# Attention and two feed-forward layers on one core: earlier splits at a pair's end, and a new division of work in the first attention batch

## The chip, the cores and the metric

The kernel runs on one core of one Trainium2 chip. The metric is device time in microseconds (us) of one execution. Engines are named as in the profile: PE is TensorE (PEld its weight loads), DVE is VectorE, ACT is ScalarE, POOL is GpSimd, SP issues the plain DMAs.

## The reference

```python
def phi(x):                                   # random features, both for q and for k
    proj = einsum('bhsd,md->bhsm', x, omega)
    h = proj - sum(x * x) / 2
    return exp(h - max(h)) / sqrt(m)
q_p, k_p = phi(q * scale), phi(k * scale)     # 4 batches, 8 heads, 576 tokens, 64 -> 128 features
kv, z = einsum('bhsm,bhsd->bhmd', k_p, v), sum(k_p, axis=2)
x = einsum('bhsm,bhmd->bhsd', q_p, kv) / (einsum('bhsm,bhm->bhs', q_p, z) + 1e-06)
x = softplus(x @ w_in) @ w_out                # 2304 tokens, 512 -> 2048 -> 512
for e in range(8):                            # each token goes to its best expert, 512 -> 1024 -> 512
    out[mask] = gate * (relu(x[mask] @ w1[e]) @ w2[e])
```

## The kernel before

**Three stages.** Attention feeds the first feed-forward layer, which takes the tokens in six groups of 384; the attention of later batches is woven between the matmuls of the first groups. The expert layer follows, from about 620 us on.

**Splitting.** Most matmuls work on two parts of a number: a rounded high part and the rest. A split is two instructions: ACT writes the high part (a cast), then DVE subtracts it from the source and writes the low part. A product is then three matmuls: high by high, high by low, low by high.

**Attention.** Work comes in items of two 128-token pieces of two heads. `u` is the half of the heads (0 or 1), `b` the batch. Stage T transposes the input and splits it (`xThi`, `xTlo`), stage P multiplies by the features (`pp`) and takes the negated row maxima (`nm`), then makes the exponentials. `TUNE['exp_k']`, one letter for each `2*b + u`, says how for the keys: with 'a', ACT makes one exponential for each 128 columns with the maximum as its bias; with 'v', DVE adds the maxima to all columns, and ACT makes one exponential over them:

```python
if TUNE["exp_" + kind][2 * b + u] == "v":
    nc.vector.tensor_tensor(out=pe[:, :2 * n], in0=ph, in1=bc(nm[:, :2 * n].unsqueeze(2), [P, 2 * n, M]),
                            op=ALU.add)
    nc.scalar.activation(out=pe[:, :2 * n], in_=pe[:, :2 * n], func=AF.Exp)
else:
    for i in range(2 * n):
        nc.scalar.activation(out=pe[:, i, :], in_=pp[:, i * M:i * M + M], func=AF.Exp, bias=nm[:, i:i + 1])
```

Stage K sums the keys by values in `kv`, and stage N multiplies the queries' features by that into `nd`: 64 rows of `nd` are numerators and 64 denominators. ACT copies the denominators to `den` (L401), and `move("nx", ...)` copies the numerators to `xf` (L252 on ACT, L254 on DVE, by `TUNE['nx']`). Stage M divides: ACT makes the reciprocal `rc`, POOL multiplies, DVE corrects (L433). The first feed-forward group (`h`, L638) waits for the `x` that this writes.

**What sets the order there.** The attention's and the feed-forward's instructions are placed by a scheduler that has its own idea of durations; each engine then runs its own list strictly in order. The order in which DVE and ACT come to their work is thus fixed when the kernel is built.

**The expert layer** is a sequence of units in an order written out by hand (all but the first). A pair unit treats two 128-token slots of one expert, a single unit one. Units 4, 6, 8, 10, 12 and 14 are pairs, and each is followed by a single. Within a unit, the code also splits the next unit's weights: `w1_(c)` splits chunk c of `w1` (128x1024, in four chunks) into the buffers that chunk c of the present unit held, `w2_(c)` one of eight of `w2`. `pair_m1(g, k)` makes a fourth of the hidden values (L1365), `split(*hidden(k), ...)` applies relu and splits them (L1241, L1242), `pair_m2(g, k)` multiplies them into the output `po` (L1376), `unit_x(g + 1)` transposes and splits the next unit's tokens (`pt_x`, `mx`), `unit_out` scales (`ot`) and writes out. A single unit begins with `slot_m1(g, 0)` (L1343): it takes the high parts of the four chunks first, each for the two parts of the tokens, then the low parts of the four chunks. L1246 is the cast of a split, L1250 its subtraction, for weights and tokens alike.

Of the kernel before, what the change touches and what calls it, by code (L numbers as in the profile page):

```python
# [24 lines left out]
    kvs='aaaaaaaa',  # L25
    zc='aaaaaaaa',
    nd='aaavvaaa',
    nx='aavaaaaa',
    xh='aapaaaaa',
    qt='vvaaaaaa',  # L30
    exp_k='vaaavaaa',
    exp_q='vavvaavv',
    xl='pppppppp',
    den='sssssvvv',
# [42 lines left out]
def tile_kernel(ctx, tc, q, k, v, omega, w_in, w_out, emb, tau, w1, w2, out):  # L77
# [1138 lines left out]
    def fetch_w(s, which="12", chain=0):  # L1216
        for nm, src in (("w1r", w1v), ("w2r", w2v)):
            if nm[1] not in which:
                continue
            if s < 2:  # L1220
                raw_w[nm, s] = mraw.tile([P, NC * F2], F32, name=f"{nm}{s}")
            with tc.issue_after(marks["x"]) if chain and "x" in marks and s < 4 else ExitStack():
                nc.gpsimd.indirect_dma_start(
                    out=raw_w[nm, s % 2], out_offset=None, in_=src,
                    in_offset=bass.IndirectOffsetOnAxis(ap=w_idx[:, s:s + 1].bitcast(U32), axis=0),
                    bounds_check=E * P - 1, oob_is_err=False)

    def fetch_x(g):
        t = xpool.tile([P, 2, YW], F32, tag="xhi", name="xg")
        for i, s in enumerate(groups[g]):  # L1230
            nc.gpsimd.indirect_dma_start(
                out=t[:, i, :], out_offset=None, in_=(ya if s < NS_A else yb)[:, :],
                in_offset=bass.IndirectOffsetOnAxis(ap=g_idx[:, s:s + 1].bitcast(U32), axis=0),
                bounds_check=NT - 1, oob_is_err=False)
            xgs[s] = t[:, i, :]
            if s >= NS_A:
                marks["x"] = traced()

    def split(hi, lo, lo_eng, src, relu=False, hi_eng="a"):
        if relu:  # L1240
            nc.scalar.activation(out=hi, in_=src, func=AF.Relu)  # L1241
            nc.vector.scalar_tensor_tensor(out=lo, in0=src, scalar=0.0, in1=hi.bitcast(F32),  # L1242
                                           op0=ALU.max, op1=ALU.subtract)
        else:
            if hi_eng == "a":
                nc.scalar.copy(out=hi, in_=src)  # L1246
            else:
                (nc.gpsimd if hi_eng == "p" else nc.vector).tensor_copy(hi, src)
            eng = nc.gpsimd if lo_eng == "p" else nc.vector
            eng.tensor_tensor(out=lo, in0=src, in1=hi.bitcast(F32), op=ALU.subtract)  # L1250
# [55 lines left out]
    def unit_w1(g, c):  # L1306
        if (g, c) in w1s:
            return
        r = raw_w["w1r", g % 2][:, c * F2:(c + 1) * F2]
        t = [wpool.tile([P, F2], F32R, tag=f"wi{2 * c + i}", name=f"w1_{c}_{i}") for i in range(2)]  # L1310
        if len(groups[g]) == 1:
            o, r = [x.rearrange("q (h p c) -> q h p c", h=2, c=4) for x in t], \
                r.rearrange("q (p h c) -> q h p c", h=2, c=4)
        else:

            o, r = [x.rearrange("q (k p j) -> q k p j", k=4, j=2) for x in t], \
                r.rearrange("q (p k j) -> q k p j", k=4, j=2)
        kind = 0 if g < 2 else len(groups[g])
        split(*o, TUNE["w1"][kind][c], r, hi_eng=TUNE["w1h"][kind][c])
        w1s[g, c] = t  # L1320

    def unit_w2(g, c):
        if (g, c) in w2s:
            return
        r = raw_w["w2r", g % 2][:, c * DM:(c + 1) * DM]
        w2s[g, c] = [wpool.tile([P, DM], F32R, tag=f"wo{2 * c + i}", name=f"w2_{c}_{i}") for i in range(2)]
        split(*w2s[g, c], TUNE["w2"][g >= 2][c], r, hi_eng=TUNE["w2h"][g >= 2][c])
# [3 lines left out]
    def hidden(key):  # L1331
        hs[key] = [ring.tile([P, 512], F32R, tag=f"wo{x}", name=f"mh_{x}") for x in "hl"]
        return hs[key]

    def slot_m1(g, half, part=slice(0, 12)):
        if part.start == 0:
            hs["ps", half] = mpsum("h", "ph")
        ph = hs["ps", half]
        w = slice(half * HF, half * HF + HF)
        mms = [(xs[g][a][c], w1s[g, c][b_][:, w]) for c, (a, b_) in first_order(half)]  # L1340
        for i in range(part.start, part.stop):
            x, r = mms[i]
            nc.tensor.matmul(ph, lhsT=x, rhs=r, start=(i == 0), stop=(i == 3 * NC - 1))  # L1343
# [14 lines left out]
    def pair_m1(g, k):  # L1358

        ph = hs["ps"] = mpsum("h", "ph")  # L1360
        order = first_order(k)
        for n, (c, (a, b_)) in enumerate(order):
            for j in range(2):
                f = slice(2 * k * P + j, 2 * (k + 1) * P, 2)
                nc.tensor.matmul(ph[:, j * 256:j * 256 + 256], lhsT=w1s[g, c][b_][:, f],  # L1365
                                 rhs=xs[g][a][c].rearrange("p i t -> p (i t)"),
                                 start=(n == 0 and j == 0), stop=(n == len(order) - 1), skip_group_check=True)

    def unit_m2(g, i, parts):

        s = groups[g][i]
        if parts[0][2] == 0:
            po[s] = mpsum("o", "po")
        for h, o, c in parts:
            for n, (a, b_) in enumerate(PASSES):
                nc.tensor.matmul(po[s], lhsT=h[a][:, o:o + P], rhs=w2s[g, c][b_], start=(c == 0 and n == 0),  # L1376
                                 stop=(c == 7 and n == 2))

    def slot_m2(g, half, cs):
        unit_m2(g, 0, [(hs[half], c * P, 4 * half + c) for c in cs])  # L1380

    def pair_m2(g, k):
        for i in range(2):
            unit_m2(g, i, [(hs[k], 256 * j + P * i, 2 * k + j) for j in range(2)])

    def unit_out(g):
        for s in groups[g]:
            xt = xgs.pop(s)
            ot = xpool.tile([P, DM], F32, tag="xlo", name="ot")
            nc.scalar.activation(out=ot, in_=po.pop(s), func=AF.Copy, scale=xt[:, DM:YW])  # L1390
            nc.gpsimd.indirect_dma_start(  # L1391
                out=out, out_offset=bass.IndirectOffsetOnAxis(ap=s_idx[:, s:s + 1].bitcast(U32), axis=0),
                in_=ot, in_offset=None, bounds_check=NT - 1, oob_is_err=False)

    def unit(g):
        nxt = g + 1 < NG_ALL
        ahead = g + 2 < NG_ALL

        def w1_(*cs):
            for c in cs:  # L1400
                if nxt:
                    unit_w1(g + 1, c)

        def w2_(*cs):
            for c in cs:
                if nxt:
                    unit_w2(g + 1, c)

        def fetch():
            if ahead:  # L1410
                fetch_x(g + 2)
                fetch_w(g + 2, "2", 1)

        def own(*cs):
            for c in cs:
                unit_w2(g, c)

        if ahead:
            fetch_w(g + 2, "1", 1)
        if len(groups[g]) == 2:  # L1420
            pair_m1(g, 0)
            own(2, 3, 4)
            split(*hidden(0), "v", hs["ps"], relu=True)
            pair_m1(g, 1)
            own(5)
            split(*hidden(1), "v", hs["ps"], relu=True)
            pair_m2(g, 0)
            pair_m1(g, 2)
            own(6, 7)
            fetch()  # L1430
            w2_(0)
            split(*hidden(2), "v", hs["ps"], relu=True)
            pair_m2(g, 1)
            pair_m1(g, 3)
            w2_(1, 2, 3)
            split(*hidden(3), "v", hs["ps"], relu=True)
            pair_m2(g, 2)
            if nxt:
                unit_x(g + 1)
            w1_(0, 1, 2, 3)  # L1440
            pair_m2(g, 3)
            unit_out(g)
            w2_(4, 5)
        else:
            if g > 0:
                slot_m1(g, 0)
            own(2, 3, 4)
            slot_relu(0)
            slot_m1(g, 1, slice(0, 5))
            own(5)  # L1450
            slot_t(0)
            slot_m1(g, 1, slice(5, 12))
            own(6, 7)
            slot_relu(1)
            slot_m2(g, 0, (0, 1))
            w1_(0)
            slot_t(1)
            slot_m2(g, 0, (2, 3))
            if nxt:
                unit_x(g + 1)  # L1460
            w1_(1, 2, 3)
            slot_m2(g, 1, (0, 1))
            if g == 2:
                tokens(bm_b, NT_T, NS_A, NS_B, mpsum("o", "Lb"))
            fetch()
            slot_m2(g, 1, (2, 3))
            unit_out(g)
            w2_(0, 1)
# [127 lines left out]
```

## Time and profile before

| | |
|---|---|
| runs, us | 946.91, 940.6, 940.16 (median 940.6) |
| profiled execution, us | 942.76 |
| its span from first to last instruction, us | 940.9 |
| PE busy | 891.9 us (95%) |
| DVE, ACT, POOL busy | 689.8, 652.8, 323.0 us |

The span is what the rows below divide up; the profiled execution's own time has 1.9 us more around it, and it lies 2.2 us above the median of the runs. Busy shares over the whole span hide the stages, so the rows below are taken by stretch.

### The profile page before, as it was taken

The page shows a single profiled execution, that of the slowest core. Times are in us where ns is not written, and L with a number is a line of the kernel's source. Part 1 is how long each engine was busy: PE and PEld are TensorE (multiplying, and loading weights), DVE is VectorE, ACT ScalarE, POOL GpSimd, SP SyncE. Part 2 cuts the span into 40 slices and gives each one's busy share as a digit, 9 for nine tenths or more (in the row PEclk, how much of TensorE's full clock was granted, in tenths as well). Part 3 has the DMA queues.
Part 4 walks back from the last instruction along what each step waited for, and adds up shares of the span by engine and source line. Part 5 has one row for each costly group of instructions (what it writes and reads, how often), then busy time and mean ns, then how long its engine had stood idle before and what let it go on. Part 6 is the DMA issues. An engine that isn't in the chain of part 4 may idle for free. (4 is left out here: it accounts for less than half of the span.)

```text
span 940.9 us, 14526 instructions
## 1 busy us (share of the span) xinstructions
PE 891.9 (95%) x4951; PEld 744.5 (79%) x4951; DVE 689.8 (73%) x1376; ACT 652.8 (69%) x1452; POOL 323.0 (34%) x341
## 2 busy tenths in 40 slices
PE   6898899999999999998999999999999999999993
PEld 6775555588898889987888889888797888988972
DVE  6769888477888887679886777767977676685772
ACT  4897344477878877775877687876867576585672
POOL 1224102155545754575653020012243242241310
PEclk9899999999999999999999999999999999999998
DMA  6625663011362231011301381102023660551910
GB/s 165 166 76 152 185 217 113 17 35 37 57 146 72 45 93 35 20 35 23 68 7 23 81 344 46 34 12 57 26 65 142 276 243 30 211 209 41 356 58 6
DMA packets 86540, 94.69 MB, mean 101 GB/s; under 512 B 50294, under 2 KB 74870, under 8 KB 84160
## 3 DMA queue, kind: packets, MB, share of 16 engines
q1 hardware_dynamic: 77888, 45.21, 18.5%
q0 software_dynamic: 8576, 48.52, 13.7%
q8 instruction: 41, 0.67, 0.3%
q14 instruction: 35, 0.29, 0.1%
HBM read 108.36 MB, written 15.48 MB: 132 GB/s over the span
## 5 line engine op out<-in xcount | busy, mean ns | idle before, releaser
L1376 PE MATMUL po<-w,mh_h 128*128 128x512 f32 x368 | 118.0, 402 | 0.5 <-ACT mh_h L1354 0.5
L1250 DVE TENSOR_TENSOR w<-w2r,w 128x512 fp32r<-128x512 f32 x136 | 88.4, 684 | 17.5 <-ACT w L1246 17.5
L703 PE MATMUL y<-woh,gh 128*128 128x512 f32 x240 | 96.2, 408 | 1.7 <-DVE gh L682 1.7
L1246 ACT CAST w<-w2r 128x512 fp32r<-128x512 f32 x136 | 78.7, 628 | 23.3 <-DMA w2r<-in_moe_w_dram,w_idx 12.8
L703 PE MATMUL y<-wol,gh 128*128 128x512 f32 x240 | 93.9, 395 | 0.0
L1391 POOL DMA_INDIRECT out_dram<-ot,s_idx x23 | 31.5, 1369 | 171.0 <-ACT ot L1390 126.5
L1250 DVE TENSOR_TENSOR w<-w1r,w 128x1024 fp32r<-128x1024 f32 x68 | 80.4, 1226 | 11.1 <-ACT w L1246 11.0
L703 PE MATMUL y<-woh,gl 128*128 128x512 f32 x240 | 81.7, 404 | 0.0
L598 DVE TENSOR_TENSOR wil<-win,wih 128x512 fp32r<-128x512 f32 x72 | 58.4, 811 | 29.1 <-ACT wih L597 28.9
L1376 PEld LDWEIGHTS po<-w,mh_h 128*128 128x128 f32 x368 | 66.9, 191 | 12.2 <-ACT mh_h L1354 0.7
L638 PE MATMUL h<-xhi,wih 128*128 128x384 f32 x320 | 73.0, 348 | 3.2 <-DVE t L657 2.9
L1246 ACT CAST w<-w1r 128x1024 fp32r<-128x1024 f32 x68 | 72.0, 1119 | 3.5 <-PE ph L1343 2.1
L1376 PE MATMUL po<-w,mh_l 128*128 128x512 f32 x184 | 73.4, 399 | 0.9 <-DVE mh_l L1356 0.9
L610 POOL TENSOR_TENSOR wol<-wout,woh 128x512 fp32r<-128x512 f32 x40 | 55.0, 1376 | 45.3 <-ACT woh L609 45.2
L638 PE MATMUL h<-xlo,wih 128*128 128x384 f32 x320 | 70.2, 337 | 0.0
L638 PE MATMUL h<-xhi,wil 128*128 128x384 f32 x320 | 69.9, 339 | 0.0
L1365 PE MATMUL ph<-mxh,w 128*128 128x256 f32 x384 | 62.6, 285 | 0.4
L638 PEld LDWEIGHTS h<-xhi,wih 128*128 128x128 f32 x320 | 55.4, 188 | 8.3 <-DVE t L657 3.7
L425 POOL TENSOR_TENSOR xf<-xf,rc 128x256 f32<-128x256 f32 (+1 forms) x20 | 17.3, 867 | 122.0 <-ACT rc L424 114.8
L638 PEld LDWEIGHTS h<-xhi,wil 128*128 128x128 f32 x320 | 57.7, 188 | 0.3
L1365 PEld LDWEIGHTS ph<-mxh,w 128*128 128x128 f32 x384 | 55.0, 195 | 2.9 <-ACT w L1246 1.6
L638 PEld LDWEIGHTS h<-xlo,wih 128*128 128x128 f32 x320 | 56.4, 188 | 0.0
(311 smaller groups left out, 2376.6 us busy)
## 6 DMA issues: line engine op xcount, KB each, us to landing
wst<-in_moe_w_in_dram SPq DMA_DIRECT2D x16, 512.0 KB, 4.5
wst<-in_moe_w_out_dram SPq DMA_DIRECT2D x16, 512.0 KB, 4.3
raw<-in_k_dram SPq DMA_DIRECT2D x32, 128.0 KB, 2.4
vf<-in_v_dram SPq DMA_DIRECT2D x64, 64.0 KB, 2.3
raw<-in_q_dram SPq DMA_DIRECT2D x32, 128.0 KB, 2.6
ya<-yt SPq DMA_DIRECT2D x20, 128.2 KB, 4.4
yb<-yt SPq DMA_DIRECT2D x20, 128.2 KB, 4.0
ya<-yt SPq DMA_DIRECT2D x8, 256.5 KB, 5.7
```

Of the source, the lines that this page charges most:

```text
L425: nc.gpsimd.tensor_tensor(out=xf, in0=xf, in1=rc, op=ALU.mult)
L598: feng("il", n).tensor_tensor(out=il, in0=wi, in1=ih.bitcast(F32), op=ALU.subtract)
L610: feng("ol", n).tensor_tensor(out=ol, in0=wo, in1=oh.bitcast(F32), op=ALU.subtract)
L638: nc.tensor.matmul(h[:, 0:G], lhsT=a[:, c, :], rhs=x[:, c, :], start=(i == 0), stop=(i == last))
L703: nc.tensor.matmul(y, lhsT=x[:, c], rhs=w, start=(f == 0 and i == 0), stop=(f == NF - 1 and i == len(passes) - 1))
L1246: nc.scalar.copy(out=hi, in_=src)
L1250: eng.tensor_tensor(out=lo, in0=src, in1=hi.bitcast(F32), op=ALU.subtract)
L1365: nc.tensor.matmul(ph[:, j * 256:j * 256 + 256], lhsT=w1s[g, c][b_][:, f], rhs=xs[g][a][c].rearrange("p i t -> p (i t)"), start=(n == 0 an ...
L1376: nc.tensor.matmul(po[s], lhsT=h[a][:, o:o + P], rhs=w2s[g, c][b_], start=(c == 0 and n == 0), stop=(c == 7 and n == 2))
L1391: nc.gpsimd.indirect_dma_start(out=out, out_offset=bass.IndirectOffsetOnAxis(ap=s_idx[:, s:s + 1].bitcast(U32), axis=0), in_=ot, in_offset ...
```

## The change

Two letters-in-a-table edits and one reordering. In batch 0, the numerators of both halves of the heads are copied by DVE instead of ACT (`nx`), and the maxima of the second half's keys are added by DVE (`exp_k`), so that ACT makes one exponential where it made four. At a pair's end, the next unit's first chunk of `w1` is split ahead of the last hidden split, the second ahead of the next unit's tokens, and the third and fourth where all four stood.

```diff
-    nx='aavaaaaa',
+    nx='vvvaaaaa',
...
-    exp_k='vaaavaaa',
+    exp_k='vvaavaaa',
...
             pair_m1(g, 3)
             w2_(1, 2, 3)
+            w1_(0)
             split(*hidden(3), "v", hs["ps"], relu=True)
             pair_m2(g, 2)
+            w1_(1)
             if nxt:
                 unit_x(g + 1)
-            w1_(0, 1, 2, 3)
+            w1_(2, 3)
             pair_m2(g, 3)
             unit_out(g)
             w2_(4, 5)
```

ACT's list at the end of a pair unit (the second one), before. `w2r` and `w1r` are the raw weights of the next unit, `mh_h` the high part of the hidden values, `mx` that of the next unit's tokens:

```order
L1246 CAST w_1_0_10240<-w2r_6603 128x512
L1246 CAST w_2_0_10244<-w2r_6603 128x512
L1246 CAST w_3_0_10248<-w2r_6603 128x512
L1241 ACTIVATE mh_h<-ph 128x512
L1246 CAST mx<-pt_x 128x512
L1246 CAST w_0_0_10276<-w1r_6599 128x1024
L1246 CAST w_1_0_10280<-w1r_6599 128x1024
L1246 CAST w_2_0_10284<-w1r_6599 128x1024
L1246 CAST w_3_0_10288<-w1r_6599 128x1024
```

The same place on ACT after the change:

```order
L1246 CAST w_1_0_10232<-w2r_6595 128x512
L1246 CAST w_2_0_10236<-w2r_6595 128x512
L1246 CAST w_3_0_10240<-w2r_6595 128x512
L1246 CAST w_0_0_10244<-w1r_6591 128x1024
L1241 ACTIVATE mh_h<-ph 128x512
L1246 CAST w_1_0_10264<-w1r_6591 128x1024
L1246 CAST mx<-pt_x 128x512
L1246 CAST w_2_0_10276<-w1r_6591 128x1024
L1246 CAST w_3_0_10280<-w1r_6591 128x1024
```

One cast of `w1r` now stands ahead of the last relu, and one between it and the tokens' cast; DVE's subtractions moved in the same way.

DVE's list where the first numerators come out of `nd`, some 32 us into the span, as a piece of the difference:

```order
 L598 TENSOR_TENSOR wil<-win_365,wih 128x512
-L288 TENSOR_REDUCE nm<-pp 128x4
-L270 TENSOR_TENSOR xTlo<-pt_k,xThi 128x256
+L254 COPY xf<-nd 64x256 x2
+L288 TENSOR_REDUCE nm<-pp 128x4
+L270 TENSOR_TENSOR xTlo<-pt_k,xThi 128x256
+L288 TENSOR_REDUCE nm<-pp 128x4
+L254 COPY xf<-nd 64x320
+L270 TENSOR_TENSOR xTlo<-pt_k,xThi 128x256
+L296 TENSOR_TENSOR kh<-pp,nm 128x512
```

The copies of `xf` and the additions (L296) are now between DVE's maxima and its halves of the splits; on ACT the copies (L252) are gone from between the `den` copies. The scheduler also placed other instructions of the attention anew; PE's list is the same again from some 90 us on, DVE's from some 165 us.

## Rows read from the trace of the kernel before

**Rows 1.** Windows of the attention stretch: us, busy by engine, clock, DMA share, GB/s.

```profile
30.00:75.00 45.00, 40.78 (x282) 33.77 (x282) 29.16 (x64) 42.67 (x135) 13.27 (x18) 0.99 0.43 111
75.00:85.00 10.00, 7.78 (x43) 5.34 (x42) 9.72 (x17) 8.40 (x25) 4.10 (x5) 1.00 0.42 128
```

**Rows 2.** Waits of PE, 30 to 85 us: total us, times, longest.

```profile
PE nd L395 <- ACT xf L252: 1.2, 2, 0.9
PE kv L318 <- ACT kh L301: 1.2, 1, 1.2
PE nd L395 <- DVE xTlo L270: 1.1, 1, 1.1
PE pp L282 <- ACT pe L301: 0.6, 1, 0.6
```

**Rows 3.** Lines by form, 20 to 200 us: numerator copies; busy us, mean ns, idle before.

```profile
L252 ACT COPY xf<-nd 64x320 f32<-64x320 f32 x8 | 3.3, 418 | 0.1
L254 DVE COPY xf<-nd 64x320 f32<-64x320 f32 x4 | 2.0, 489 | 1.7 <-ACT den L401 1.6
L254 DVE COPY xf<-nd 64x256 f32<-64x256 f32 x4 | 1.7, 417 | 0.1
...
L252 ACT COPY xf<-nd 64x256 f32<-64x256 f32 x8 | 2.9, 367 | 0.1
```

**Rows 4.** Timeline of ACT, then lines by form of 20 to 200 us: exponentials, additions.

```profile
41.42 1.15 ACT L301 ACTIVATE kh<-pp,nm 128x128 f32<-128x128 f32 x4
...
L296 DVE TENSOR_TENSOR pe<-pp,nm 128x512 f32<-128x512 f32 x12 | 8.2, 684 | 0.7 <-PE pt_q L365 0.6
...
L298 ACT ACTIVATE pe<-pe 128x512 f32<-128x512 f32 x12 | 7.6, 630 | 17.2 <-DVE pe L296 17.2
```

**Rows 5.** Timeline of PE where singles begin: start, us, operation, idle before.

```profile
711.69 1.65 PE L1343 MATMUL ph<-w,mx 128*128 128x512 f32 x6
713.55 1.43 PE L1343 MATMUL ph<-w,mx 128*128 128x512 f32 x5 [0.21 <-ACT w L1246]
715.37 1.66 PE L1343 MATMUL ph<-w,mx 128*128 128x512 f32 x6 [0.39 <-DVE w L1250]
...
899.91 1.65 PE L1343 MATMUL ph<-w,mx 128*128 128x512 f32 x6
...
913.67 4.21 PE L1343 MATMUL ph<-w,mx 128*128 128x512 f32 x17
```

**Rows 6.** Timeline of ACT at the end of the first pair.

```profile
702.34 1.30 ACT L1246 CAST w<-w2r 128x512 fp32r<-128x512 f32 x2 [0.96 <-PE po L1376]
705.90 0.60 ACT L1241 ACTIVATE mh_h<-ph 128x512 fp32r<-128x512 f32 x1 [2.25 <-PE ph L1365]
709.12 0.59 ACT L1246 CAST mx<-pt_x 128x512 fp32r<-128x512 f32 x1 [2.62 <-PE pt_x L1265]
709.60 3.90 ACT L1246 CAST w<-w1r 128x1024 fp32r<-128x1024 f32 x4
713.40 1.26 ACT L1390 ACTIVATE ot<-po,xg 128x512 f32<-128x512 f32 x2
...
715.91 0.60 ACT L1347 ACTIVATE hs<-ph 128x512 f32<-128x512 f32 x1 [0.22 <-PE ph L1343]
```

**Rows 7.** Timeline of DVE at the end of the first pair.

```profile
706.53 0.69 DVE L1242 SCALAR_TENSOR_TENSOR mh_l<-ph,mh_h 128x512 fp32r<-128x512 f32 x1 [2.15 <-ACT mh_h L1241]
709.74 0.69 DVE L1250 TENSOR_TENSOR mx<-pt_x,mx 128x512 fp32r<-128x512 f32 x1 [2.52 <-ACT mx L1246]
710.68 4.63 DVE L1250 TENSOR_TENSOR w<-w1r,w 128x1024 fp32r<-128x1024 f32 x4 [0.25 <-ACT w L1246]
```

**Rows 8.** Timeline of ACT in the second pair: a wait for weights to land.

```profile
736.13 0.62 ACT L1246 CAST w<-w2r 128x512 fp32r<-128x512 f32 x1 [2.19 <-DMA w2r<-in_moe_w_dram,w_idx]
737.92 0.60 ACT L1241 ACTIVATE mh_h<-ph 128x512 fp32r<-128x512 f32 x1 [1.17 <-PE ph L1365]
```

**Rows 9.** DMA issues between 719 and 721 us, for the next single: us to landing last.

```profile
w1r<-in_moe_w_dram,w_idx POOLq DMA_INDIRECT x1, 9.4
```

## The prediction

> **What bounds the kernel now.** The chain of waits that ended last reaches back only into the tail, so it says nothing of the changed places, and I read by stretch instead: first the windows, to see which engine is full where; then the waits of PE there; then the timelines of the engines that PE waits for. PE is busy 95% of the span, so what can be won is its idle time and little else.
>
> Two places of that kind are touched. In the attention stretch from 30 to 75 us, ACT is busy 42.67 of 45 us and DVE 29.16; PE is idle for 45 - 40.78 = 4.2 us, and for another 10 - 7.78 = 2.2 us up to 85 us [rows 1]. So ACT is the full engine up to 75 us; from there DVE is (9.72 of 10). Of PE's longer waits, those that name ACT (numerators copied, keys' and queries' exponentials) add up to 1.2 + 1.2 + 0.6 = 3.0 us, against 1.1 us for a split's low part on DVE [rows 2].
>
> At the start of a single unit behind a pair, PE stops twice in its first twelve matmuls: the seventh waits for the high part of the fourth chunk, the twelfth for its low part. Seventeen matmuls take from 711.69 to 715.37 + 1.66 = 717.03 us, that is 5.34 us; in the last single, which follows another single, the same seventeen take 4.21 us [rows 5]. The loss is 1.13 us, and its cause is in the rows of ACT and DVE: the four casts run back to back from 709.60 to 713.50, the four subtractions from 710.68 to 715.31 [rows 6, 7], and PE goes on 0.05 us after the last of each. This happens six times, every 37.64 us (711.69 and 899.91 are the first and the last).
>
> **The change at a pair's end.** Nothing is added or removed: 4 casts and 4 subtractions of each pair stand earlier in two lists. A cast takes 3.90 / 4 = 0.98 us in such a run, a subtraction 4.63 / 4 = 1.16 us.
>
> The first cast now stands ahead of the last hidden relu. ACT is done with the `w2` casts at 703.64 and then idle for 2.25 us until the relu at 705.90 [rows 6]; the chunk's buffer is free once PE has passed chunk 0 in the matmuls that the relu waits for, so the cast fits in that gap and costs nothing. Without that cover (the buffer free only at the end of those matmuls) the relu would come 1.0 us later and its subtraction end near 708.4 instead of 707.22; PE wants them after 708.8 (twelve matmuls of 0.23 us before 711.69), so this too would be hidden. On DVE the first subtraction falls into 2.15 us of idleness before 706.53, the second into the 2.52 us before 709.74 [rows 7]; the second cast falls into ACT's 2.62 us before 709.12. Left behind the tokens are two casts, 709.60 to 711.6, and two subtractions, from 710.7 to 713.0. PE wants the fourth high part with its seventh matmul at 711.69 + 6 x 0.23 = 713.1 and the fourth low part with the twelfth at 714.2. Both waits go, with over 1 us to spare.
>
> What is late next: the relu of the single (`hs`) needs PE's twelfth matmul, about 714.8. ACT's queue ahead of it is two scalings (1.26 us, now from 711.6 or, for the second slot, from PE's last output near 712.1) and two `w2` casts (1.30 us by the pair in [rows 6]), done by 714.7 at the latest. The raw `w1` is no new wait: for the second pair it is issued near 720 and has landed 9.4 us later [rows 9], while the moved cast comes near 741 (703.6 and 37.6). The raw `w2` is closer: ACT waits 2.19 us for it in the second pair, and the relu behind it has 1.17 us left before PE needs it [rows 8]. If PE runs 1.13 us earlier and the landing stayed, that would just do; and the loads stand on POOL's queue behind the write of `ot`, whose scaling moves from 713.40 to about 711.6, more than PE moves.
>
> Sum for the pairs: 6 x 1.13 = **6.8 us** gained.
>
> **The change in batch 0.** Sixteen numerator copies leave ACT: 8 x 0.367 + 8 x 0.418 = 6.3 us [rows 3]. Eighteen exponentials of 128 columns become four of 512 and one of 256: 1.15 us for four against 0.63 for one, 4.5 times, is 2.3 us [rows 4]. So ACT loses 8.6 of its 42.67 us. DVE gets the copies at 8 x 0.417 + 8 x 0.489 = 7.3 us, by the rows of batch 1 that are already copied there [rows 3], and 4.5 additions of 0.684 = 3.1 us [rows 4]; 10.4 us in all, which brings it to 39.5 of 45 us, while ACT falls to 34.1. No DMA is added. Each copy and addition stands in DVE's list between maxima and low parts for which PE's projections wait, so behind a waiting copy those wait too; the first four fall at 31 to 36 us.
>
> The price on the path isn't shown in the trace, so it is bounded. At best all of PE's idle time up to 85 us goes, 6.4 us [rows 1]. At worst the new work on DVE is all on the path and ACT's relief is not: a loss of 10.4 us. I take 3.0 us gained, the waits that name ACT [rows 2], and leave those on DVE as they are: PE's 40.78 us set a floor which DVE's 39.5 us still lie under, so DVE becomes the second engine, close behind, and not the first. Everything after is placed by data and buffers, not by a clock, so what is won at 75 us should be kept; a few tenths more or less may come from the scheduler's new order up to 165 us.
>
> On copying out of PSUM, the row has 417 and 489 ns on DVE against 367 and 418 ns on ACT [rows 3]. The Trainium skill says in "VectorE: DVE Perf Modes", Specifications, that VectorE sits closer to SBUF and ScalarE closer to PSUM, which speaks against moving such copies, and the trace agrees by 50 to 71 ns a copy. If that difference lay on the path, the sum would be 16 x 0.06 = 1.0 us worse, an estimate from the rows; by the rows' idle time on DVE it is hidden.
>
> **Sum.** 942.76 - 6.8 - 3.0 = 933.0 us for the profiled execution; that one lay 2.2 us above the median of its runs, so against the median 940.6 the forecast is **930.8 us**, 1.04% faster.
>
> **Rivals.** (1) The attention gives nothing: PE's waits change their name from ACT to DVE, which is nearly full as well. For it: 39.5 us of DVE work against a floor of 40.78; against it: DVE was idle for 16 of 45 us, much of it while it waited for ACT. Time 940.6 - 6.8 = 933.8 us. (2) The attention gives all of PE's idle time: 940.6 - 6.8 - 6.4 = 927.4 us. For it: ACT falls by a fifth; against it: some waits there name loads and DVE. (3) The pairs' wait moves to the landing of raw `w2` [rows 8]: from the second pair on, each gives its 1.13 us back there, which leaves 1.13 of 6.8 us: 940.6 - 1.1 - 3.0 = 936.5 us. Against it, the loads' issue moves with the unit. (4) Slower: DVE in batch 0 is a chain (low part, projection, maxima, addition, exponential), and its idle time there is waiting for its own products, so that none of the 10.4 us is hidden: 940.6 + 10.4 - 6.8 = 944.2 us. It decides against the change once over 6.8 of the 10.4 us lie on the path. Against it: the idle rows of DVE name ACT. (5) The change does not do what it says, the splits start no sooner: then only the attention's 3.0 us are left, 937.6 us.
>
> **How the numbers follow.** About 1% (9.4 us, so 931.2 us) is what a measurement of this kernel can tell from no change. The forecast has 0.45 (between 929.3 and 932.3 us), rival 1 0.24 (932.3 to 935.3), rival 2 0.18, rival 3 and 5 together 0.08, rival 4 0.05. The range 926.5 to 936 us takes in the first three whole and leaves out most of the rest. Faster by over 1% is rival 2 and some 0.27 of the forecast: 0.45. Within 1% is the other 0.18 of it with rivals 1, 3 and 5: 0.50. Slower by over 1% is at most rival 4: 0.05.
>
> **What will show it.** Pairs: no idle time on PE in the first seventeen matmuls of the six singles (4.2 us each), one cast of `w1` between 703 and 706 us of this time axis. Attention: ACT near 34 us in the stretch that was 30 to 75 us, DVE near 39, the first `h` matmul some 3 us before 72.9. The prediction is wrong if DVE is full there and PE waits for `xTlo`, `nm` or `xf`, or if ACT's waits for `w2r` grow and the relu behind them comes late.

## The result, and the profile after

The changed kernel takes 930.84 us (median of four runs, 929.19 to 931.36), beside 941.49 us for the kernel before: 10.65 us less by the medians. The ratio, worked out from all runs and not from the two medians, is 0.9877, 95% interval 0.9856 to 0.9898, or 11.6 us (9.6 to 13.6). The profiled execution took 930.39 us, its span is 928.6 us, 12.3 us less than before.

The windows of the attention stretch, as in [rows 1] (busy by engine, clock, DMA share, GB/s):

```profile
30.00:75.00 45.00, 42.11 (x300) 36.16 (x300) 40.58 (x91) 38.30 (x113) 14.95 (x20) 1.00 0.44 112
75.00:85.00 10.00, 9.73 (x45) 6.82 (x46) 9.86 (x18) 8.35 (x27) 3.08 (x3) 1.00 0.71 211
```

PE's idle time falls from 4.22 + 2.22 = 6.4 us to 2.89 + 0.27 = 3.2 us. ACT is at 38.30 and not near 34, because more of the program now falls into the stretch (300 matmuls for 282). Up to the first `h` matmul, which comes at 72.92 us before and at 69.31 after, the windows are, before and after:

```profile
30.00:72.92 42.92, 38.70 (x275) 32.54 (x274) 27.15 (x60) 40.61 (x130) 12.49 (x17) 0.99 0.42 110
30.00:69.31 39.31, 36.55 (x267) 31.95 (x267) 34.97 (x78) 33.87 (x101) 13.03 (x18) 1.00 0.47 119
```

There ACT has 29 instructions fewer and 6.7 us less to do (the prediction counted 8.6), and DVE 7.8 us more (it counted 10.4), with 267 matmuls ahead of that point for 275. The waits of PE from 30 to 85 us, as in [rows 2], after the change:

```profile
PE pt_q L377 <- DVE xf L254: 0.8, 1, 0.8
PE pp L282 <- DVE pe L296: 0.7, 1, 0.7
PE h L638 <- ACT t L655: 0.4, 1, 0.4
PE kv L318 <- ACT kl L298: 0.3, 1, 0.3
PE pt_k L266 <- DVE nm L288: 0.3, 1, 0.3
PE pt_k L262 <- DVE xTlo L270: 0.3, 1, 0.3
PE pp L282 <- DVE kh L296: 0.3, 1, 0.3
```

The 3.0 us that named ACT's numerators and exponentials are down to 0.3 us. Before, the waits that name DVE were the 1.1 us of [rows 2] and one more,

```profile
PE h L638 <- DVE x L433: 0.6, 1, 0.6
```

so they have grown from 1.7 to 2.4 us.

PE at the start of the first two singles behind a pair, and of the last single, which follows a single, as in [rows 5]:

```profile
707.84 4.02 PE L1343 MATMUL ph<-w,mx 128*128 128x512 f32 x17
...
744.14 4.02 PE L1343 MATMUL ph<-w,mx 128*128 128x512 f32 x17
...
901.80 4.22 PE L1343 MATMUL ph<-w,mx 128*128 128x512 f32 x17
```

The seventeen matmuls stand in one row with no idle time: 4.02 us where they took 5.34. The period of the units is 36.30 us for 37.64. ACT at the first pair's end, as in [rows 6] (in brackets the idle time before an instruction and what ended it):

```profile
699.89 1.05 ACT L1246 CAST w<-w1r 128x1024 fp32r<-128x1024 f32 x1
702.05 0.60 ACT L1241 ACTIVATE mh_h<-ph 128x512 fp32r<-128x512 f32 x1 [1.10 <-PE ph L1365]
702.54 1.05 ACT L1246 CAST w<-w1r 128x1024 fp32r<-128x1024 f32 x1
705.27 0.59 ACT L1246 CAST mx<-pt_x 128x512 fp32r<-128x512 f32 x1 [1.68 <-PE pt_x L1265]
705.75 2.00 ACT L1246 CAST w<-w1r 128x1024 fp32r<-128x1024 f32 x2
...
710.76 0.60 ACT L1347 ACTIVATE hs<-ph 128x512 f32<-128x512 f32 x1 [0.81 <-PE ph L1343]
```

and DVE, as in [rows 7]:

```profile
700.97 1.22 DVE L1250 TENSOR_TENSOR w<-w1r,w 128x1024 fp32r<-128x1024 f32 x1 [0.46 <-ACT w L1246]
...
703.62 1.23 DVE L1250 TENSOR_TENSOR w<-w1r,w 128x1024 fp32r<-128x1024 f32 x1 [0.25 <-ACT w L1246]
...
706.83 2.36 DVE L1250 TENSOR_TENSOR w<-w1r,w 128x1024 fp32r<-128x1024 f32 x2 [0.25 <-ACT w L1246]
```

Behind each moved cast ACT still waits for PE (1.10 and 1.68 us): the casts lie in its idle time. The last subtraction ends at 709.19, and PE's twelfth matmul starts near 707.84 + 11 x 0.23 = 710.4.

**Where the 12.3 us of span came from.** Four rows of PE of the two kernels, the first matmul of the first layer's second group (L638) and the first of the expert layer (L1343). Before:

```profile
190.51 0.94 PE L638 MATMUL h<-xhi,wih 128*128 128x384 f32 x4
...
622.71 0.39 PE L1343 MATMUL ph<-w,mxh 128*128 128x512 f32 x1
```

After:

```profile
187.59 0.94 PE L638 MATMUL h<-xhi,wih 128*128 128x384 f32 x4
...
620.36 0.39 PE L1343 MATMUL ph<-w,mxh 128*128 128x512 f32 x1
```

The attention's lead is 3.6 us at the first `h` matmul (69.31 for 72.92), 2.9 at the second group and 2.35 at the expert layer. At the first single behind a pair it has become 711.69 - 707.84 = 3.85 us, 1.5 more, for a reason that the edits don't settle (the clock, last section). The six pairs add 6 x 1.32 = 7.9, and the rest, some 0.5 us, comes behind the last.

### The profile page after: what moved, and what is told of

It is laid out like the page before. It is cut to its first block, busy times and chain, and to the rows that moved or that the text cites. A ratio compares the mean times of both kernels' runs of the same rounds, so it can differ in the third digit from the quotient of the medians.

```text
span 928.6 us, 14509 instructions
## 1 busy us (share of the span) xinstructions
PE 885.2 (95%) x4951; PEld 744.5 (80%) x4951; DVE 699.9 (75%) x1397; ACT 644.9 (69%) x1423; POOL 323.0 (35%) x341
## 5 line engine op out<-in xcount | busy, mean ns | idle before, releaser
L1391 POOL DMA_INDIRECT out_dram<-ot,s_idx x23 | 35.0, 1522 | 162.8 <-ACT ot L1390 122.0
L638 PE MATMUL h<-xhi,wih 128*128 128x384 f32 x320 | 73.0, 348 | 3.2 <-DVE t L657 2.9
L638 PE MATMUL h<-xlo,wih 128*128 128x384 f32 x320 | 70.3, 337 | 0.0
L638 PE MATMUL h<-xhi,wil 128*128 128x384 f32 x320 | 70.0, 339 | 0.0
L638 PEld LDWEIGHTS h<-xhi,wih 128*128 128x128 f32 x320 | 55.4, 188 | 8.4 <-DVE t L657 3.7
L638 PEld LDWEIGHTS h<-xhi,wil 128*128 128x128 f32 x320 | 57.7, 188 | 0.3
L638 PEld LDWEIGHTS h<-xlo,wih 128*128 128x128 f32 x320 | 56.4, 188 | 0.0
L282 PE MATMUL pp<-obd_hi,xThi 128*128 128x256 f32 x144 | 49.4, 343 | 6.9 <-DVE pe L296 6.1
```

The source lines that it names most:

```text
L282: nc.tensor.matmul(o, lhsT=hi[:, c], rhs=obd_hi, start=True, stop=False)
L638: nc.tensor.matmul(h[:, 0:G], lhsT=a[:, c, :], rhs=x[:, c, :], start=(i == 0), stop=(i == last))
L1391: nc.gpsimd.indirect_dma_start(out=out, out_offset=bass.IndirectOffsetOnAxis(ap=s_idx[:, s:s + 1].bitcast(U32), axis=0), in_=ot, in_offset ...
```

## The experiments

In all of them the ratio is to the kernel before, timed on the same chip beside it, with the 95% interval.

**The pair's end alone.** The new `unit()` with the two tables as before.

```diff
-    nx='vvvaaaaa',
+    nx='aavaaaaa',
-    exp_k='vvaavaaa',
+    exp_k='vaaavaaa',
```

> The code of the pair's end as changed, the attention's two strings as before. Theory (the two parts are independent and add up; the pair part is worth the whole stop at the singles' start, 5.34 - 4.02 = 1.32 us, six times 7.9): a ratio of 0.9916 (941.5 - 7.9 = 933.6 us); singles' starts 36.3 us apart instead of 37.64. Rival 1 (the prediction's size, 6 x 1.13 = 6.8 us): 0.9928, 934.7 us. Rival 2 (part of what the pairs seemed to win, the 1.6 us between the first expert matmul and the first pair, belongs to this code too): 932.0 us, 0.990.

Measured: 934.93 us, 0.9919 (0.9900 to 0.9938), or 7.6 us. The singles behind pairs start at 711.93 and 748.24 us, 36.31 apart, with 4.02 and 4.03 us for the seventeen. The theory's 7.9 us and the prediction's 6.8 are both inside the interval; the rows speak for 7.9. Rival 2 falls: the expert layer's first stretch was no shorter.

**The attention alone.** The two tables as changed, `unit()` as before.

> The attention's two strings as changed, the pair's end as before. Theory (independent parts; 3.6 us sooner at the first h matmul, of which about 2.9 are left at the first matmul of the second group): ratio 0.997 (938.6 us), singles' starts 37.64 us apart. Rival (what the attention wins is given back altogether in the first group, which the conversion of the weights on DVE paces, and the pairs hold all of the gain): 1.000, 941.5 us. A second rival (all 3.6 us and the 1.6 us between the first expert matmul and the first pair come from here): 0.9945, 936.3 us.

Measured: 939.64 us, 0.9979 (0.9966 to 0.9991), 2.0 us (0.8 to 3.2). Both extremes fall. The parts add up to 9.6 us, the two together measured 1 - 0.9877 = 11.6 us (9.6 to 13.6).

**Its halves.** First the numerators alone, then the keys' maxima alone (each is one of the two table lines).

> The numerators of batch 0 on DVE alone (nx), the keys' exponentials and the pair's end as before: 6.3 us of ACT's work go. Theory (relief of ACT counts in proportion: 6.3 of 8.6 us): 2.1 of 2.9 us, ratio 0.9978, 939.4 us. Rival 1 (only the waits of PE that name the numerators, 1.2 of 3.0 us): 0.9987, 940.3 us. Rival 2 (the scheduler's new order makes the gain and the parts don't add up): this and the next run don't sum to the gain of the two together.

> The keys' maxima of half the heads of batch 0 added by DVE alone (exp_k), numerators and the pair's end as before: 2.3 us of ACT's work go, 3.1 us come to DVE. Theory (relief of ACT in proportion: 2.3 of 8.6 us): 0.8 of 2.9 us, ratio 0.9992, 940.7 us. Rival 1 (the waits of PE that name the keys' exponentials, 1.2 of 3.0 us, go): 0.9987, 940.3 us. Rival 2 (not additive, the scheduler's order decides): a loss, or the whole 2.9 us.

Measured: the numerators 939.60 us, 0.9978 (0.9964 to 0.9991), as much as both halves together. The keys' maxima: 949.01 us, **1.0072** (1.0052 to 1.0092), a loss of 6.8 us. No theory had that size. The two do not add up, so I looked at the lists of the built kernels. PE's 5100 instructions (matmuls and weight loads) stand as in the kernel before from the 527th on with the numerators alone and from the 467th on with both edits, but with the keys' maxima alone only from the 2828th on. In between, the scheduler has set the later batches' attention one chunk of the first layer (12 `h` matmuls) earlier: the third batch's first `nd` stands behind 172 `h` matmuls instead of 184. The rows of that kernel show where the loss is:

```profile
192.80 0.94 PE L638 MATMUL h<-xhi,wih 128*128 128x384 f32 x4
...
629.61 0.39 PE L1343 MATMUL ph<-w,mxh 128*128 128x512 f32 x1
```

2.3 us are lost ahead of the second group, and 4.6 us behind its start, where no edited instruction stands any more (436.8 us from one row to the other, 432.2 before).

**Order and operations apart.** Another small edit, when the router's set-up work (a dozen small operations) is recorded, tips the scheduler the same way or back. Three kernels: the keys' maxima with the old order, the kernel before with the losing order, the changed kernel with the losing order.

```diff
 # keys' maxima alone; changed kernel
-    setup=2,
+    setup=4,
 # kernel before
-    setup=2,
+    setup=3,
```

> The exponentials' edit alone (exp_k), as in the run that lost 7 us, but the router's small set-up work is put two chunks later (setup=4 for 2), which makes the scheduler fall back into the kernel before's order of the matmuls from the 511th of 5100 on; the first 431 stand as in the losing run. Theory (the loss is the scheduler's other order, which set the later batches' attention one chunk of the first layer earlier, not the exponentials): the loss goes; ratio 0.998 to 1.002 (940 to 944 us). Rival (the additions on DVE cost the time themselves): 1.007, 949 us as before.

> The kernel before with nothing but the router's set-up one chunk later (setup=3 for 2), by which the scheduler takes the order of the losing run: the matmuls stand alike from the 636th of 5100 on. No operation moves to another engine. Theory (that order costs what the losing run lost behind the first group, 629.6 - 192.8 against 622.7 - 190.5, 4.6 us): ratio 1.005, 946.5 us. Rival (the order is harmless, the operations cost): 1.000, 941.9 us.

> The changed kernel with nothing but the router's set-up two chunks later (setup=4 for 2), by which the scheduler takes the order of the losing run from the 636th matmul on; the first 431 stand as in the changed kernel. Theory (the order's price doesn't hang on the engines' division of work): 4.6 us slower than the changed kernel, 935.5 us, ratio 0.9932. Rival (only with ACT full does the order cost): 930.9 us, 0.988.

Measured: 1.0007 (0.9993 to 1.0021), 1.0076 (1.0057 to 1.0095) and 0.9932 (0.9914 to 0.9950). The theory's cause holds in all three: the keys' maxima cost nothing that can be measured when the order stays, the order costs 7.2 us (5.4 to 9.0) with no operation moved between engines, and 5.2 us (0.9932 - 0.9877) in the changed kernel. Its size was too small for the second: 4.6 us lie outside that interval, because the theory counted only what the losing run lost behind the start of the second group. That set-up work moved by two chunks is harmless in itself is the first run's result; moved by one chunk it was not run in the old order, but the losing order costs 6.8 us with the set-up work in its old place too. The rows of the kernel before in the losing order:

```profile
194.48 0.94 PE L638 MATMUL h<-xhi,wih 128*128 128x384 f32 x4
...
632.11 0.39 PE L1343 MATMUL ph<-w,mxh 128*128 128x512 f32 x1
```

The second group starts 4.0 us later than before, and 437.6 us lie between the two rows, 5.4 more than before. PE's longest waits from 190 to 620 us, first of the kernel before, then of this one:

```profile
PE h L638 <- DVE t L657: 2.9, 2, 1.6
PE y L703 <- DVE gh L682: 1.7, 2, 1.2
```

```profile
PE y L703 <- DVE gh L682: 2.8, 7, 0.6
PE h L638 <- DVE t L657: 2.7, 4, 1.2
```

PE stops more often, seven times for `gh` instead of two. But its idle time there is only 2.0 us longer (9.2 for 7.2); how the other 3.4 us come about, in rows that read as busy, stays open. The granted clock is 1.00 throughout that stretch, so it isn't the clock. Behind it the clock does add 1.5 us in this profiled execution, the slowest of the kernel's five runs: from the first expert matmul to the first pair it takes 67.1 us, where the kernel before takes 65.6 (last section). That doesn't carry the ratio, since the mean granted clock of the five runs, 0.989 to 0.991, is no lower than in the runs of the kernel before beside it (0.985 to 0.992).

**A third order.** The version of the next paragraph with the set-up one chunk later, by which attention of the second and third batch stands later.

> The changed kernel with the single units' earlier split too, and the router's set-up one chunk later (setup=3), by which the scheduler takes a third order: the second batch's and third batch's attention stand up to one chunk of the first layer later than in the kernel before, from the 2206th matmul on as there. Theory (what costs is attention that stands earlier than the products it needs): not slower than the run without it, 0.984 to 0.985. Rival (the kernel before's order is the best of the three, any shift costs): 4 us slower, 0.989.

Measured: 931.42 us, 0.9887 (0.9868 to 0.9907), some 4 us slower than without it. The second group starts sooner (185.16 us), the expert layer later (623.75). "Later is harmless" falls; of the three orders the one of the kernel before is the best. The two profiled executions can't be compared row by row, because the clock falls at other places: from the first expert matmul to the first pair it is 65.2 us here and 63.6 without.

**The same cure for the single units.**

```diff
             slot_m2(g, 0, (2, 3))
+            w1_(1)
             if nxt:
                 unit_x(g + 1)
-            w1_(1, 2, 3)
+            w1_(2, 3)
```

> The changed kernel, and in the single units the second chunk of w1 is split ahead of the next unit's tokens too. Theory (the small stop at each pair's start, about 0.2 us for the third chunk of w1, goes as the larger one at the singles' start did): six or seven times 0.2, 1.2 us faster than the changed kernel, 929.6 us, ratio 0.9868. Rival 1 (a pair's first matmuls need the tokens first, which now come about 1 us later): the same number of times about 0.5 us slower, 934 us. Rival 2 (no difference): 930.8 us, 0.988.

Measured: 928.32 us, **0.9843** (0.9825 to 0.9862), the lowest ratio here; its interval is apart from the kernel before's by a wide margin, and overlaps the changed kernel's by little. I expected 1.2 us and got some 3 (0.9877 - 0.9843). Behind pairs, PE's rows read

```profile
706.47 4.02 PE L1343 MATMUL ph<-w,mx 128*128 128x512 f32 x17
...
742.35 4.03 PE L1343 MATMUL ph<-w,mx 128*128 128x512 f32 x17
```

35.88 us apart, 0.42 less than after the change: the small stop at each pair's start is worth twice the 0.2 us that I had read. It hardly shows as idle time: the first 28 matmuls of a pair take 3.74 us after the change (from 720.74 us) and 3.35 us here, and of the 0.39 us only 0.03 are idle time of PE; the rest stands in rows that read as busy. The last single, which took 4.22 us, now takes 4.01. A stop of 0.40 us in a unit ahead of the pairs (658.82 us after the change) went as well.

**One chunk instead of two** (attention as before).

```diff
             pair_m2(g, 2)
-            w1_(1)
             if nxt:
                 unit_x(g + 1)
-            w1_(2, 3)
+            w1_(1, 2, 3)
```

> The attention as before; of the pair's end only the first chunk of w1 is split ahead of the hidden relu, the second stays behind the tokens. Theory (deadlines: with three casts from 709.6 us the fourth high part is there at 712.5 and PE wants it at 713.1; the fourth low part at 714.2, wanted at 714.2): nearly the whole 7.9 us, 934.5 us, ratio 0.992, as with two chunks. Rival (each chunk that is moved gives its share): half, 4 us, 938.5 us, ratio 0.9958.

Measured: 933.65 us, 0.9923 (0.9905 to 0.9941), as good as two chunks (0.9919). PE at the first single:

```profile
709.58 4.22 PE L1343 MATMUL ph<-w,mx 128*128 128x512 f32 x17
```

4.22 us: 1.12 of the 1.32 us are gained by the first chunk, 0.20 by the second. It goes by deadlines, not by shares.

**Is it DVE's conversion that takes back part of the lead?** The third operation of the conversion is left out.

```diff
-        nc.vector.scalar_tensor_tensor(out=o, in0=lo, scalar=29, in1=o,
-                                       op0=ALU.logical_shift_right, op1=ALU.bitwise_or)
         yield
```

> The changed kernel without the third operation of the weights' conversion (L564): the lowest three bits of the first layer's weights are left out. DVE has 17.7 us less to do between 85 and 165 us; the matmuls stand in the changed kernel's order from the 547th on. Theory (DVE's conversion paces the first group, which is why 3.6 us at its start are 2.9 us at its end): the second group's first matmul some 4 us sooner, 926.5 us, ratio 0.984. Rival (the loads of the raw weights pace it, by 411 KB a us at best and the waits of DVE for them): under 1 us sooner, 930 us, 0.9875.

Measured: 930.95 us, 0.9887 (0.9867 to 0.9907), no gain over the changed kernel. In the profile the second group starts at 186.01 us, 1.6 sooner and not the 4 of the theory, which falls; the rival's "under 1 us" isn't met there either. DVE's waits for raw weights between 69 and 190 us, first after the change, then without that operation:

```profile
DVE win L558 <- DMA wst<-in_moe_w_in_dram: 5.8, 7, 1.7
DVE wout L558 <- DMA wst<-in_moe_w_out_dram: 3.4, 6, 1.4
```

```profile
DVE win L558 <- DMA wst<-in_moe_w_in_dram: 8.3, 9, 1.7
DVE wout L558 <- DMA wst<-in_moe_w_out_dram: 7.2, 9, 1.3
```

With less to do, DVE waits 6.3 us longer for loads, and longer for ACT as well (`t`, 12.5 us for 8.4, and `gf`, 8.6 for 5.1). So DVE's conversion paces little of that group; whether the loads or ACT pace it was not tried.

**Without the keys' maxima, but with all the rest.**

> Numerators on DVE, pair's end and single units with earlier splits, but the keys' exponentials as before (no exp_k). Theory (exp_k is worth nothing by itself, since the run with the numerators alone measured as the two together): as the run with all three, ratio 0.985. Rival (with the numerators gone from ACT, the exponentials' edit gives the rest of the 2.9 us): 0.6 us or more slower than that run, 0.9855 or more.

Measured: 927.33 us, 0.9858 (0.9837 to 0.9878), not to be told from the run with them (0.9843, 0.9825 to 0.9862). The number just reaches the rival's 0.9855, so the rival's 0.6 us isn't ruled out, only too small for these runs. In no run is the `exp_k` edit worth anything that can be measured.

## Why the prediction was right

**Total.** Forecast 930.8 us, measured 930.84. Two errors cancel: the pairs give about 1 us more than forecast, and the median that the gain was taken from, 940.6 us, lies 0.9 us below the one measured with the changed kernel, 941.49. So the agreement to 0.04 us is luck; that the forecast's ratio (930.8 / 940.6 = 0.9896) lies inside the interval is not.

**Pairs, 6.8 us: right mechanism, too small.** All the steps that the prediction named are in the rows: both casts in ACT's gaps, the fourth chunk ready 1.2 us ahead of its use, the single's relu waiting 0.81 us for PE and not PE for it. The term measured 6 x 1.32 = 7.9 us in the rows, 7.6 in time. The mis-sized step is "in the last single the same seventeen take 4.21 us": that single has a short stop of its own. It still takes 4.22 us after the change, and a single whose second chunk isn't moved takes just that (4.22), while one with nothing to wait for takes 4.02; with the single units' split it takes 4.01. Seventeen matmuls at the 0.23 us that the prediction used elsewhere, 3.9 us, would have shown it.

**Rival 3 (raw `w2`).** ACT in the second pair, as in [rows 8]:

```profile
729.82 0.62 ACT L1246 CAST w<-w2r 128x512 fp32r<-128x512 f32 x1 [1.06 <-DMA w2r<-in_moe_w_dram,w_idx]
...
732.73 0.60 ACT L1241 ACTIVATE mh_h<-ph 128x512 fp32r<-128x512 f32 x1 [2.29 <-PE ph L1365]
```

The wait is 1.06 us where it was 2.19, and the relu's room 2.29 where it was 1.17. The prediction's reason fits: the loads stand on POOL's queue behind the write of `ot`, whose scaling on ACT ends at 707.65 + 1.27 = 708.92 us now.

**Attention, 3.0 us.** In time 2.0 us alone (0.8 to 3.2) and 11.6 - 7.6 = 4.0 us as the difference of the whole and the pairs; in PE's idle time up to 85 us, 3.2. The first is known to 1.2 us, the second to some 3. So 3.0 was a fair size; rival 1 (nothing) and rival 2 (6.4 us) lie outside the interval of the run alone. The rule behind the 3.0 (waits that name ACT go, those on DVE stay) held about so: 2.7 us went, 0.7 came, with the wait for `x` counted that the prediction left out. What was wrong is the division: the prediction counted the 2.3 us of exponentials as relief, and their edit alone gave nothing in time (1.0007 in the old order). As far as the runs can tell, the numerators carry the gain. The relief of the exponentials is real as far as the first `h` matmul, though: with their edit alone in the old order that one comes at 69.05 us, 3.9 sooner than before, and with the numerators alone at 69.11, each as soon as with both (69.31). But the second group then starts at 191.24 and 189.33 us for 190.51, so a lead at the first `h` matmul isn't yet a gain; in the one profile it was all lost in the first group. DVE did not become a chain (rival 4): PE still waits for it for 2.4 us only.

**The step that held for a reason it didn't name.** "A few tenths more or less may come from the scheduler's new order" holds for this kernel because PE's list falls back into the old one at the 467th instruction. That it does had been seen, from some 90 us on, but the prediction put no price on a list that does not. The keys' maxima without the numerators give such a list, and cost 6.8 us. The rival that ended slower should have been this one: three runs show the losing order at 5 to 7 us, and a fourth another order at 4. The order itself could be compared before any time was known; its price could not.

**"What is won at 75 us should be kept."** In the profile 3.6 us became 2.35 up to the expert layer. With the attention alone, whose lists are those of the changed kernel up to the first pair's end, the lead was 2.1 us at the first `h` matmul (70.85), 2.5 at the second group (187.99) and 2.3 at the expert layer (620.45): nothing was lost. The changed kernel's own loss in the first group may be the clock, which falls there in its profile and not in the other (last section), or scatter between executions: two kernels with the attention of before reach the second group at 190.8 and 188.55 us (pair's end alone, one chunk), where before did at 190.51. How much of a lead is kept is not settled to better than some 2 us.

## What to carry to other kernels

Where a scheduler makes the lists, compare the whole list of the engine that bounds, not only the edited place: see from which instruction on it is the same again, and treat an edit that leaves it different for thousands of instructions as another kernel; a harmless edit elsewhere can put the old order back, and so tell order from operation. Work that several consumers wait for in turn goes by deadlines: moving the first of four splits into an idle gap brought 1.12 of 1.32 us. And take the reference for "no wait" from a count of instructions times their spacing, not from another place of the kernel that may wait as well.

## What the runs showed that I had not expected

**A fall of PE's clock worth 1.5 us.** In the profile of before the granted clock falls while PE is busy, in the router's stretch (5.00 of 5 us in the window of the fall):

```profile
630.00:635.00 5.00, 4.46 (x27) 3.38 (x26) 4.70 (x5) 4.52 (x8) 0.03 (x1) 1.00 0.00 0
635.00:640.00 5.00, 5.00 (x34) 4.71 (x34) 2.08 (x11) 4.06 (x12) 0.96 (x1) 0.80 0.02 2
```

A mean of 0.80 lies between full speed, 2.4 GHz, and the half of it, 1.2: part of the window was at the lower level. After the change the same work, 2.35 us earlier and behind the same 4.46 us of PE work in 5 us, keeps the full clock:

```profile
627.65:632.65 5.00, 4.46 (x27) 3.37 (x26) 4.71 (x5) 4.52 (x8) 0.03 (x1) 1.00 0.00 0
632.65:637.65 5.00, 5.00 (x38) 4.69 (x38) 2.07 (x11) 4.57 (x13) 0.96 (x1) 1.00 0.01 0
```

In the changed kernel's profile it falls in the first group instead, in a window with 1.9 us of waiting:

```profile
110.00:115.00 5.00, 3.11 (x5) 1.40 (x6) 4.81 (x14) 0.15 (x1) 0.00 (x0) 0.76 0.59 183
```

From the first expert matmul to the first pair it is 65.6 us before and 64.0 after. Of the 14 profiles, 11 show the fall in the router's stretch; only the changed kernel, the one with the single units' split and the one without the third conversion do not. In two kernels with the losing order (the kernel before's and the changed kernel's operations) it falls for longer, and the stretch takes 67.1 us. The same lists can go either way: in the run with the attention alone all lists are those of the changed kernel up to the first pair's end, yet its clock falls in the router's stretch, and the way to the first pair takes 65.6 us:

```profile
635.00:640.00 5.00, 5.00 (x21) 4.17 (x21) 3.76 (x16) 3.56 (x10) 0.00 (x0) 0.66 0.00 0
```

What decides between the two, no run here shows. It is the 1.5 us by which the two profiled executions differ more than the edits explain.
